# Block-sparse attention and expert layer: sampled value rows of every second group fetched by whole-block transfers, neighbour value rows copied by engines, and a planner with other durations

## The chip, the cores and the metric

The kernel runs on one core of a Trainium2 chip, as one program. Its engines are TensorE (PE, with its weight loads as PEld), VectorE (DVE), ScalarE (ACT), GpSimd (POOL) and SyncE (SP), which here does nothing but issue transfers; 16 DMA engines move the data. Each engine works through its own instructions in the order in which they were written, and waits where one of them waits. The metric is the device time of one execution in microseconds (us).

## The reference

The first half is block-sparse attention over 4 batches of 8 heads, 768 rows in 24 blocks of 32. A row of queries sees its own block and both neighbours, the first and the last block, and three sampled blocks out of a table that comes in as data. The first and the last block of queries see every key.

```
mask = np.abs(blk_i - blk_j) <= 1
mask = mask | (blk_i == 0) | (blk_j == 0) | (blk_i == 23) | (blk_j == 23)
for qb in range(24):
    for kb in sampled_blocks[qb]:
        mask[qb*32:(qb+1)*32, kb*32:(kb+1)*32] = True
attn = softmax(where(mask, scale * q @ k.T, -1e9)) ; out = attn @ v
```

The second half is an expert layer over the 3072 rows of that output (512 wide): a greedy assignment of 384 rows to each of 8 experts by their logits, and `relu(x @ w1[e]) @ w2[e]` for the rows of each.

## The kernel before, in words

The attention runs first (about 340 us of the span), then the choice of the first expert, then the expert layer (class `Moe`). The change is in the attention (class `Attn`) and in the planner (class `Plan`) that sets its order; the instructions of the expert layer keep theirs.

A batch has 24 blocks of queries. Blocks 1 to 22 go in groups of four, u = 0 to 5 (the last has two); the first and the last block go apart (kind "D"), against all keys. In each batch the kernel does this:

- `keys` loads each 128-row chunk of k and q from HBM into a staging tile `st` (SP, L245), transposes it on PE into `S` (L253), and copies it into `kT` or `qT` (ACT or DVE).
- `values` loads v into `vn` (SP, L275) and writes the rows back to HBM as `vrows` (SP, L279), so that they can be fetched by row number.
- `group_keys` puts the keys that a group sees side by side in `kg` (two buffers, used by turns: kg0 for even u, kg1 for odd u): first, last and neighbour blocks by ACT or POOL (L227 on POOL), the sampled blocks by 12 copies on POOL (L338) whose source is a block number read into registers (L333).
- `group_values` puts the values of a group into two tiles: `vw` (two buffers), with the first block and the neighbours, by copies (ACT or POOL) and by transfers from `vn` (SP, L371 to L419); and `vz` (three buffers: u modulo 3), with the sampled blocks, by one indirect gather for each block of queries from `vrows` (POOL, L360: 96 rows of 2080 bytes, by the row numbers in `vidx`), and with the last block (SP, L365). A sampled block that the row sees anyway is fetched from a row of zeros behind `vrows`.
- `pair` multiplies queries with `kg` into `S` (L473; 16 such products are one unit); `unit` takes the smallest and subtracts it (DVE, L514 and L519), transposes (PE, L533), takes the exponential into `aT` (ACT, L539) and multiplies with `vw` and `vz` (PE, L558); `quotient` divides and writes the rows out.

Every piece is a task of `Plan`: a priority (its place on a time scale of 30 to the batch), the engine or engines that may do it with a duration each (microseconds), the tasks it depends on, the buffers it takes, and for a transfer its time on the DMA engines (`move`). `Plan.run` goes through time with these durations and writes each task's instructions when it comes up, so the durations decide the order on every engine and which of ACT, POOL or DVE does a copy. They decide nothing at run time: there each engine takes its instructions in that order, and semaphores hold it until its inputs are there. SP's transfers come out in the planned order too.

Of the kernel before, what the change touches and what calls it, by code (L numbers as in the profile page):

```python
# [24 lines left out]
class Plan:  # L25
# [7 lines left out]
    def __init__(self):  # L33
        self.tasks, self.pools, self.rows = [], {}, {}
# [57 lines left out]
    def run(self, look=0.25, window=9.0):  # L92
# [45 lines left out]
class Attn:  # L138
# [20 lines left out]
    def consts(self):  # L159
# [13 lines left out]
        zero = self.kg[1][0:1].rearrange("p a b c -> p (a b c)")[:, 0:VR]  # L173
        nc.vector.memset(zero, 0.0)
        for b in range(self.nb):
            nc.scalar.dma_start(self.vs[b][S:S + 1], zero)
# [4 lines left out]
    def rows(self):  # L181
# [25 lines left out]
        for r in range(3):  # L207
            sl = slice(32 * r, 32 * r + 32)
            nc.vector.tensor_scalar(row[sl], self.tbl[sl, :, r], float(BS), y[sl], op0=OP.mult, op1=OP.add)
            nc.vector.tensor_scalar(to[sl], row[sl], -1.0, float(S), op0=OP.mult, op1=OP.add)  # L210
            nc.vector.scalar_tensor_tensor(to[sl], had[sl, :, r], 0.5, to[sl], op0=OP.is_ge, op1=OP.mult)
            nc.vector.tensor_tensor(self.vidx[sl], row[sl], to[sl], op=OP.add)
        self.sum4 = T("sum4", [128, E])
# [19 lines left out]
    def keys(self, b, at, ahead):  # L233
# [4 lines left out]
        for (nm, c), n in at:  # L238
# [21 lines left out]
            ld = pl.add(n - ahead, ("SP", 0.5), load, take=[st], move=1.2)  # L260
            self.kld[key] = ld
            a = pl.add(n, ("PE", 0.52), turn, deps=[ld], after=first[nm], take=[ps] + ([] if first[nm] else [sl]), use=[st])
# [3 lines left out]
    def values(self, b, n0, step):  # L266

        nc, pl = self.nc, self.plan
        self.vnslot[b] = s = pl.slot("vn")
        self.rel[b], lds = [], []  # L270
        behind = [] if b else [self.kld[0, "q", 1]]
        vn = self.vn[b % 2]
        for c in range(6):
            def load(c=c):
                nc.sync.dma_start(vn[:, c, :, 0:D], self.v[b, :, 128 * c:128 * c + 128].rearrange("h p d -> p h d"))  # L275
            lds.append(pl.add(n0 + c * step, ("SP", 0.5), load, deps=[self.base], after=lds[:1] + behind, take=[s] if c == 0 else [], use=[s], move=1.2))
            if c % 2:
                def rows(c=c):
                    nc.sync.dma_start(self.vs[b][128 * (c - 1):128 * (c + 1)].rearrange("(c p) x -> p c x", p=128),  # L279
                                      vn[:, c - 1:c + 1].rearrange("p c h d -> p c (h d)"))  # L280
                self.rel[b].append(pl.add(n0 + (c + 1) * step, ("SP", 0.5), rows, deps=lds[-2:], use=[s], move=1.5))
        self.vld[b] = lds

    def group_keys(self, b, u, n):
# [55 lines left out]
        add(("POOL", 0.4 + 0.3 * 3 * len(self.blocks(u))), f)  # L340
        self.kgt[b, u] = ts

    def group_values(self, b, u, n):
# [14 lines left out]
        for g in range(len(bl)):  # L358
# [3 lines left out]
            az(("POOL", 0.95), f, self.rel[b] + [self.idx], move=0.56, late=0.1 * g)  # L362
# [31 lines left out]
        def f():  # L394
            nc.sync.dma_start(vw[32:64, 1], vn[32:64, u])
        aw(("SP", 0.5), f, [u], move=0.2)
# [8 lines left out]
        else:  # L405
# [8 lines left out]
            def f():  # L414
                nc.sync.dma_start(vw[0:32, 2], vn[0:32, u + 1])
            aw(("SP", 0.5), f, [u + 1], move=0.2)

            def f():
                nc.sync.dma_start(vw[0:64, 3], vn[0:64, u + 1])  # L419
            aw(("SP", 0.5), f, [u + 1], move=0.4)  # L420
# [61 lines left out]
    def unit(self, x, n, qs_, avs, avd):  # L482
# [42 lines left out]
        for c0 in range(0, w, 4):  # L525
# [8 lines left out]
            tr = pl.add(n + 1, ("PE", .125 * (c1 - c0) + .02), f, deps=sub, take=[sp], use=[ss])  # L534
# [27 lines left out]
        avd.append(pl.add(n + 2.6, ("PE", 0.66), f, deps=ex + vd + avd, take=[] if s else [avs], use=[sa] + vs, row="AV"))  # L562

    def quotient(self, b, kind, u, m, n, avs, avd):
# [67 lines left out]
        t = pl.add(n + 2, ("PE", .52), f, deps=done, take=[sp], use=[xs])  # L632
# [36 lines left out]
    def run(self, start=None):  # L669
        self.st, self.T, self.ps, self.ev, self.Tslot = {}, {}, {}, {}, {}  # L670
        self.vnslot, self.rel, self.vld, self.vslot, self.vt = {}, {}, {}, {}, {}
        self.kgslot, self.kgt, self.avt, self.xslot, self.xstate, self.fin, self.lgt, self.qd0, self.kld = {}, {}, {}, {}, {}, {}, {}, {}, {}
# [705 lines left out]
def tile_kernel(tc, q, k, v, sampled_blocks, moe_w_gate, moe_w1, moe_w2, out):  # L1378
    nc = tc.nc
    with ExitStack() as ctx:  # L1380
# [10 lines left out]
        with ExitStack() as a:  # L1391
            vs = [dram.tile([S + 1, VR], F32, name=f"vrows{b}") for b in range(B)]
# [32 lines left out]
```

## Time and profile before

| | |
|---|---|
| median of 3 runs | 688.36 us (687.7 to 689.5) |
| profiled execution: its own time | 689.25 us |
| its span, first to last instruction | 687.5 us |
| busy share of the span: PE, DVE, ACT, POOL | 85%, 64%, 51%, 60% |
| mean granted TensorE clock | 0.929 of full speed |
| DMA: bytes moved, packets | 107.57 MB, 126280 |

A row of a timeline begins with the start and the duration in us; in brackets at its end stands how long the engine had stood idle before it and what released it. "issue" means that the profile shows nothing that was waited for. Stretches of equal instructions are merged into one row, x8 meaning eight of them; a merged row lasts from the first start to the last end.

### The profile page before, as it was taken

How to read it: one execution, taken by the hardware profiler on the slowest of the kernel's cores; microseconds unless marked ns; L12 is line 12 of the kernel's file. 1: busy time of each engine (PE TensorE's matmuls, PEld its weight loads, DVE VectorE, ACT ScalarE, POOL GpSimd, SP SyncE). 2: the span in 40 equal slices, each digit the busy share in tenths (PEclk: the TensorE clock that was granted, in tenths of full speed). 3: DMA queues.
4: the chain of work that ended last, by engine and by line, in shares of the span. 5: the costliest groups of instructions: out<-in, count | busy, mean ns of one | idle time of the engine just before them, and what ended most of it. 6: DMA issues, size and time to landing. Idle time of an engine off the chain costs nothing. (4 is left out here: it accounts for less than half of the span.)

```text
span 687.5 us, 19795 instructions
## 1 busy us (share of the span) xinstructions
PE 584.4 (85%) x7416; PEld 443.6 (65%) x7416; DVE 436.8 (64%) x1645; ACT 351.8 (51%) x828; POOL 412.7 (60%) x765
## 2 busy tenths in 40 slices
PE   4768798798988797987613999999999999999996
PEld 2445565475555565564403778878787878889895
DVE  3565576676756668684578787878777787633020
ACT  3644366354634456352443747566665766346341
POOL 4475567546674675856101858576676767867661
PEclk9697999999989999998855999999999999999999
DMA  9999966998599746432103554353635363645301
GB/s 180 239 212 210 259 153 187 212 267 180 139 217 263 176 132 160 121 102 84 62 0 110 182 184 154 129 173 112 213 105 178 111 211 120 201 168 170 126 13 46
DMA packets 126280, 107.57 MB, mean 156 GB/s; under 512 B 81252, under 2 KB 99812, under 8 KB 126184
## 3 DMA queue, kind: packets, MB, share of 16 engines
q1 hardware_dynamic: 116032, 76.05, 42.4%
q0 software_dynamic: 9472, 30.16, 15.3%
q8 instruction: 58, 0.95, 0.6%
q14 instruction: 38, 0.31, 0.1%
q10 hardware_dynamic: 680, 0.10, 0.1%
HBM read 76.38 MB, written 18.98 MB: 139 GB/s over the span
## 5 line engine op out<-in xcount | busy, mean ns | idle before, releaser
L789 POOL TENSOR_TENSOR wlo<-raw,whi 128x512 fp32r<-128x512 f32 x128 | 161.7, 1288 | 57.7 <-ACT whi L789 57.0
L360 POOL DMA_INDIRECT vz<-vrows,vidx x88 | 81.9, 931 | 37.9 <-issue 13.9
L514 DVE TENSOR_REDUCE mn<-S 128x2 f32<-128x512 f32 x88 | 60.1, 684 | 59.7 <-PE S L473 59.6
L539 ACT ACTIVATE aT<-pT 128x512 f32<-128x512 f32 x88 | 51.9, 596 | 71.0 <-PE pT L533 61.3
L338 POOL COPY kg<-kT 128x128 f32 x264 | 63.6, 289 | 33.8 <-issue 27.1
L473 PE MATMUL S<-kg,qT 64*32 64x256 f32 x1408 | 65.5, 419 | 15.3 <-POOL kg L338 13.6
L789 PE MATMUL po<-whi,hh 128*128 128x512 f32 x192 | 77.4, 403 | 0.0
L789 PE MATMUL po<-whi,hl 128*128 128x512 f32 x192 | 76.9, 401 | 0.0
L789 PE MATMUL po<-wlo,hh 128*128 128x512 f32 x192 | 76.5, 398 | 0.0
L789 ACT ACTIVATE whi<-raw 128x512 fp32r<-128x512 f32 x128 | 74.1, 621 | 0.1
L558 PE MATMUL av<-vw,aT 128*32 128x65 f32 x1408 | 53.1, 230 | 11.7 <-issue 7.0
L519 DVE TENSOR_TENSOR s<-S,mn 128x512 f32<-128x512 f32 x88 | 60.4, 687 | 1.8
L789 DVE SCALAR_TENSOR_TENSOR hl<-ph,hh 128x384 fp32r<-128x384 f32 x64 | 35.3, 552 | 39.8 <-ACT hh L789 39.8
L533 PE MATMUL pT<-ident,s 128*128 128x128 f32 x352 | 57.6, 288 | 1.6 <-ACT aTD L539 0.8
L789 PE MATMUL ph<-xhi,whi 128*128 128x384 f32 x256 | 58.4, 345 | 0.4 <-ACT xhi L789 0.3
L789 PE MATMUL ph<-xhi,wlo 128*128 128x384 f32 x256 | 57.9, 343 | 0.0
L789 PE MATMUL ph<-xlo,whi 128*128 128x384 f32 x256 | 57.7, 343 | 0.0
L558 PEld LDWEIGHTS av<-vw,aT 128*32 128x32 f32 x1408 | 33.1, 111 | 34.1 <-issue 21.4
L789 ACT ACTIVATE hh<-ph 128x384 fp32r<-128x384 f32 x64 | 31.2, 487 | 45.6 <-PE ph L789 43.8
L558 PE MATMUL av<-vz,aT 128*32 128x65 f32 x1408 | 49.3, 224 | 2.4 <-issue 1.9
L253 PE MATMUL S<-ident,st 128*128 128x128 f32 x192 | 33.9, 307 | 20.1 <-DMA st<-in_k_dram 9.0
L473 PEld LDWEIGHTS S<-kg,qT 64*32 64x32 f32 x1408 | 25.6, 112 | 38.7 <-POOL kg L338 24.0
(225 smaller groups left out, 1239.4 us busy)
## 6 DMA issues: line engine op xcount, KB each, us to landing
raw<-in_moe_w_dram SPq DMA_DIRECT2D x64, 512.0 KB
vrows<-vn SPq DMA_DIRECT2D x12, 520.0 KB
st<-in_k_dram SPq DMA_DIRECT2D x24, 256.0 KB
st<-in_q_dram SPq DMA_DIRECT2D x24, 256.0 KB
vn<-in_v_dram SPq DMA_DIRECT2D x24, 256.0 KB
xrows<-xt SPq DMA_DIRECT2D x20, 256.0 KB
vw<-vn SPq DMA_DIRECT2D x76, 65.0 KB
vz<-vn SPq DMA_DIRECT2D x12, 260.0 KB
```

Source lines behind the costliest of these rows:

```text
L253: nc.tensor.transpose(ps[:, 128 * p:128 * p + 128], self.st[key][:, 2 * p:2 * p + 2].rearrange("p h d -> p (h d)"), self.ident)
L338: nc.gpsimd.tensor_copy(kg()[:, :, g, 128 + 32 * r:160 + 32 * r], kT()[:, :, bass.ds(pv[3 * g + r] * BS, BS)])
L360: nc.gpsimd.indirect_dma_start(out=vz[0:96, g], out_offset=None, in_=self.vs[b], in_offset=bass.IndirectOffsetOnAxis(ap=self.vidx[:, bl[g] ...
L473: nc.tensor.matmul(x["S"][0][32 * g:32 * g + 32, 256 * j:256 * j + 256], qT[h, p, BS * bl[gi]:BS * bl[gi] + BS], kg[h, p, gi], start=True, ...
L514: nc.vector.tensor_reduce(x["mn"][:, 0:2], x["S"][0].rearrange("p (j y) -> p j y", j=2), axis=AX.X, op=OP.min)
L519: nc.vector.tensor_tensor(x["s"].rearrange("p (j t) y -> p j (t y)", j=2), x["S"][0].rearrange("p (j y) -> p j y", j=2), x["mn"][:, 0:2, N ...
L533: nc.tensor.transpose(ps[:, c - c0], x["s"][:, c], self.ident)
L539: nc.scalar.activation(x["aT"][:, c0:c1], x["ps", c0][:, 0:c1 - c0], AF.Exp, scale=-1.0 if w == 4 else 1.0)
L558: nc.tensor.matmul(av[32 * g:32 * g + 32, 2 * j + s], aT[:, 2 * j + t, 32 * g:32 * g + 32], v[:, gi, h], start=t == 0, stop=t == 1)
L789: return f(*args, **kw)
```

## The change

1. Sampled values of the odd groups (u = 1, 3, 5): instead of a gather for each block of queries on POOL (10 in a batch) SP issues three transfers of a whole sampled block, 32 rows, for each (30 in a batch). The block numbers come from a table `tz` in which a block that is seen anyway is replaced by block 24; they are read into registers on SP once for each group, in the first batch, and kept. Behind `vrows` stand 32 rows of zeros now, not one.
2. Neighbour values: three transfers of SP for a group (two of 32 rows and one of 64) become three copies by ACT or POOL, whichever the planner picks. The transfers of the first block (u = 0 and 1) stay.
3. Loads: of the first batch, the last three chunks of q may start only after `vrows` is written; the first loads of the second batch only after those.
4. The planner: other durations (the gather 1.22 for 0.95, the loads 1.35 for 1.2, and others), 2 us more behind a transfer for what depends on it, a look-ahead of 0.1 for 0.25.

```
         for d in t["deps"]:
-            at = max(at, d["end"])
+            at = max(at, d["end"] + (self.late if d["move"] and d["prio"] > 0 else 0.0))
+        if "SP" in t["eng"] and t["prio"] > 0:
+            at += self.late / 2
...
-    def run(self, look=0.25, window=9.0):
+    def run(self, look=0.1, window=9.0):
...
-            ld = pl.add(n - ahead, ("SP", 0.5), load, take=[st], move=1.2)
+            ld = pl.add(n - ahead, ("SP", 0.5), load, take=[st], move=1.35)
...
-        add(("POOL", 0.4 + 0.3 * 3 * len(self.blocks(u))), f)
+        add(("POOL", 0.8 + 0.245 * 3 * len(self.blocks(u))), f)
...
-        for g in range(len(bl)):
+        for g in range(len(bl)) if u % 2 else ():
+            def f(g=g):
+                if u not in self.kept:
+                    self.kept[u] = nc.values_load_multi_w_load_instructions(
+                        self.tz[0:1, bl[0]:bl[-1] + 1].rearrange("p n r -> p (n r)"), engines=[ET.SP], min_val=0, max_val=NB,
+                        skip_runtime_bounds_check_because="the table is clamped on the chip")[1]
+                for r in range(3):
+                    nc.sync.dma_start(vz[32 * r:32 * r + 32, g], self.vs[b][bass.ds(self.kept[u][3 * g + r] * BS, BS)])
+            az(("SP", 1.6 if b or g else 3.2), f, self.rel[b] + [self.idx], move=0.75, late=0.1 * g)
+        for g in range(len(bl)) if u % 2 == 0 else ():
             def f(g=g):
                 nc.gpsimd.indirect_dma_start(out=vz[0:96, g], out_offset=None, in_=self.vs[b],
                                              in_offset=bass.IndirectOffsetOnAxis(ap=self.vidx[:, bl[g]:bl[g] + 1], axis=0))
-            az(("POOL", 0.95), f, self.rel[b] + [self.idx], move=0.56, late=0.1 * g)
+            az(("POOL", 1.22), f, self.rel[b] + [self.idx], move=0.8, late=0.1 * g)
...
-        def f():
-            nc.sync.dma_start(vw[32:64, 1], vn[32:64, u])
-        aw(("SP", 0.5), f, [u], move=0.2)
+        def f(e):
+            self.copy(e, vw[32:64, 1], vn[32:64, u])
+        aw(both(.62, .64), f, [u])
...
-                nc.sync.dma_start(vw[0:32, 2], vn[0:32, u + 1])
-                nc.sync.dma_start(vw[0:64, 3], vn[0:64, u + 1])
+                self.copy(e, vw[0:32, 2:4], vn[0:32, u + 1, None].to_broadcast([32, 2, VR]))
+                self.copy(e, vw[32:64, 3], vn[32:64, u + 1])
...
+                for c in (2, 3, 4):
+                    self.kld[0, "q", c]["after"].append(self.rel[0][-1])
+                if b == 1:
+                    for t in [self.kld[1, "k", 0], self.vld[1][0]]:
+                        t["after"].append(self.kld[0, "q", 4])
```

Over the program the copies into `vw` go from 27 to 50 on POOL and from 45 to 86 on ACT, the gathers into `vz` on POOL from 88 to 48; SP loses 64 transfers and gains 120. Three places of the new order follow; names are those of the tiles, with buffer numbers where several exist.

PE in the first batch, up to its first product with values (`vw_99`, `vz_101` are those of u = 0, `st` is a staged chunk of k or q). Before:

```order
L473 MATMUL S<-kg_98,qT 32x256 x16
L253 MATMUL S<-ident,st 128x128 x4
L533 MATMUL pT<-ident,s 128x128 x8
L253 MATMUL S<-ident,st 128x128 x4
L533 MATMUL pT<-ident,s 128x128 x4
L473 MATMUL S<-kg_98,qT 32x256 x16
L533 MATMUL pT<-ident,s 128x128 x4
L253 MATMUL S<-ident,st 128x128 x4
L558 MATMUL av<-vw_99,aT 32x65 x4
```

After:

```order
L548 MATMUL pT<-ident,s 128x128 x4
L488 MATMUL S<-kg_98,qT 32x256 x16
L548 MATMUL pT<-ident,s 128x128 x4
L259 MATMUL S<-ident,st 128x128 x4
L573 MATMUL av<-vw_99,aT 32x65 x4
```

Three chunks of the second batch's k stood ahead of the first value product, now one does; one unit of scores (16 products with `kg_98`) and three groups of transposes of `s` moved behind it as well.

POOL in the third batch, between the sampled keys of u = 3 (`kg_98`) and those of u = 4 (`kg_97`); `vz_101` is for u = 3, `vz_102` for u = 4, `vw_100` for u = 3. Before:

```order
L360 DMA vz_101<-vrows_70,vidx 96x520 x4
L227 COPY vw_100<-vn_104 96x520
L227 COPY vw_100<-vn_104 32x520
L360 DMA vz_102<-vrows_70,vidx 96x520 x2
L227 COPY kg_97<-kT 128x4x96
L227 COPY kg_97<-kT 128x4x2x32
L227 COPY kg_97<-kT 128x4x32
L333 TENSOR_LOAD tbl
```

After:

```order
L233 COPY vw_100<-vn_104 96x520
L233 COPY vw_100<-vn_104 64x1040
L233 COPY vw_100<-vn_104 32x520
L375 DMA vz_102<-vrows_70,vidx 96x520
L233 COPY kg_97<-kT 128x4x96
L233 COPY kg_97<-kT 128x4x2x32
L233 COPY kg_97<-kT 128x4x32
L339 TENSOR_LOAD tbl
```

Five of six gathers are gone from in front of the keys of u = 4, and one copy of 64 rows by 1040 is new there.

SP in the first batch, where the second batch's fifth and sixth chunk of k are loaded; before, three transfers of neighbour values (L395 to L419) follow later:

```order
L279 DMA vrows_69<-vn_105 128x2x520
L245 DMA st<-in_k_dram 128x8x64
L275 DMA vn_105<-in_v_dram 128x8x64
L245 DMA st<-in_k_dram 128x8x64
L365 DMA vz_103<-vn_104 32x4x520
L245 DMA st<-in_q_dram 128x8x64
```

After, with `vz_101` now for u = 3 (of its 12 transfers, each behind an ISA row, the first and the last are shown):

```order
L251 DMA st<-in_k_dram 128x8x64
L281 DMA vn_105<-in_v_dram 128x8x64
L367 TENSOR_LOAD tz
L371 ISA
L371 DMA vz_101<-vrows_68 32x520
...
L371 DMA vz_101<-vrows_68 32x520
L285 DMA vrows_69<-vn_105 128x2x520
L251 DMA st<-in_k_dram 128x8x64
```

The sixth chunk of k now stands behind a register load and 12 block transfers.

## Rows read from the trace of the kernel before

**Rows 1.** Busy time of each engine by stretch: the opening, the rest of the first batch, and the three other batches. Columns: stretch, its length, PE, PEld, DVE, ACT, POOL busy us (instructions), granted TensorE clock, mean busy share of the 16 DMA engines, GB/s.

```profile
0.00:55.00 55.00, 33.76 (x364) 22.00 (x364) 27.23 (x67) 25.65 (x57) 31.40 (x92) 0.83 1.01 210
55.00:108.00 53.00, 44.88 (x1099) 31.82 (x1097) 33.13 (x81) 30.73 (x63) 28.03 (x137) 0.92 0.87 199
108.00:186.00 78.00, 68.35 (x1464) 46.09 (x1464) 56.77 (x130) 42.71 (x93) 48.98 (x119) 0.98 0.87 201
186.00:266.00 80.00, 68.91 (x1427) 45.57 (x1428) 52.27 (x118) 38.89 (x82) 50.41 (x121) 0.91 0.81 190
266.00:340.00 74.00, 60.09 (x1368) 39.52 (x1366) 48.70 (x125) 30.96 (x63) 43.06 (x98) 0.91 0.39 109
```

**Rows 2.** Waits of PE's products and weight loads in the first 340 us: who waited for whom, us in total, times, longest.

```profile
PE S L473 <- POOL kg L338: 13.6, 6, 4.2
PE S L253 <- DMA st<-in_k_dram: 9.0, 3, 6.5
PEld S L473 <- POOL kg L338: 24.0, 24, 4.3
PEld av L558 <- ACT aT L539: 8.0, 11, 1.5
```

**Rows 3.** Timeline of PE around its first value product, and the stretch just behind its longest wait (columns as in Rows 1).

```profile
44.97 0.66 PE L253 MATMUL S<-ident,st 128*128 128x128 f32 x4 [1.71 <-DMA st<-in_k_dram]
54.19 1.11 PE L253 MATMUL S<-ident,st 128*128 128x128 f32 x4 [6.51 <-DMA st<-in_k_dram]
55.23 0.44 PE L558 MATMUL av<-vw,aT 128*32 128x65 f32 x8
54.00:60.00 6.00, 5.81 (x132) 3.95 (x132) 1.31 (x4) 1.68 (x3) 2.05 (x9) 0.50 1.09 198
```

**Rows 4.** Timelines of SP and POOL in the opening: the three late loads of q, the last write of `vrows`, the third load of k of the second batch; the sampled keys of u = 1 and the first gather.

```profile
19.02 3.58 SPq L245 DMA_DIRECT2D st<-in_q_dram  x3
31.78 0.58 SPq L279 DMA_DIRECT2D vrows<-vn  x1
39.57 2.89 SPq L245 DMA_DIRECT2D st<-in_k_dram  x1
24.40 2.89 POOL L338 COPY kg<-kT 128x128 f32 x12
35.80 1.13 POOL L360 DMA_INDIRECT vz<-vrows,vidx  x1 [8.52 <-DMA vw<-vn]
```

**Rows 5.** Timeline of POOL in the third batch, from the sampled keys of u = 3 to those of u = 4.

```profile
222.81 2.88 POOL L338 COPY kg<-kT 128x128 f32 x12 [4.04 <-issue]
225.85 0.95 POOL L360 DMA_INDIRECT vz<-vrows,vidx  x1 [0.16 <-issue]
227.10 0.92 POOL L360 DMA_INDIRECT vz<-vrows,vidx  x1 [0.30 <-PE pT L533]
...
234.50 0.62 POOL L227 COPY vw<-vn 32x520 f32<-32x520 f32 x1 [3.40 <-DMA vz<-vrows,vidx]
...
237.60 1.08 POOL L227 COPY kg<-kT 128x384 f32<-128x384 f32 x3
240.05 2.89 POOL L338 COPY kg<-kT 128x128 f32 x12 [1.37 <-issue]
```

**Rows 6.** Timeline of PE: one unit of scores that waited for nothing, then those that waited for sampled keys (u = 4 of the second, third and fourth batch, and u = 1 of the fourth).

```profile
269.80 1.09 PE L473 MATMUL S<-kg,qT 64*32 64x256 f32 x32
160.11 3.18 PE L473 MATMUL S<-kg,qT 64*32 64x256 f32 x32 [0.31 <-POOL kg L338]
240.87 4.04 PE L473 MATMUL S<-kg,qT 64*32 64x256 f32 x32 [3.73 <-POOL kg L338]
314.69 4.04 PE L473 MATMUL S<-kg,qT 64*32 64x256 f32 x32 [4.19 <-POOL kg L338]
276.06 3.53 PE L473 MATMUL S<-kg,qT 64*32 64x256 f32 x32 [3.14 <-POOL kg L338]
```

**Rows 7.** Groups of instructions on POOL and ACT in the first 340 us: shapes xcount, then busy us and mean ns of one, then idle time before them.

```profile
L360 POOL DMA_INDIRECT vz<-vrows,vidx x88 | 81.9, 931 | 37.9 <-issue 13.9 <-DMA vw<-vn 8.5 <-PE av L558 7.0
L227 POOL COPY vw<-vn 32x520 f32<-32x520 f32 x15 | 9.3, 618 | 31.3 <-DMA vz<-vrows,vidx 21.0 <-PE S L253 4.8 <-PE av L558 3.5
L227 POOL COPY vw<-vn 64x1040 f32<-64x1040 f32 x2 | 2.1, 1050 | 7.4 <-PE pT L533 4.8 <-PE pT L649 2.6
L223 ACT ACTIVATE vw<-vn 64x1040 f32<-64x1040 f32 x18 | 19.2, 1068 | 5.9 <-PE av L558 5.7
L223 ACT ACTIVATE vw<-vn 32x520 f32<-32x520 f32 x17 | 10.8, 633 | 0.3
```

**Rows 8.** Timeline of SP in the second batch (the load of the third batch's fifth chunk of k, a transfer of neighbour values) and PE's transpose of that chunk; then the transfers of SP in the expert layer whose address comes from a register, two stretches of four.

```profile
141.04 0.84 SPq L245 DMA_DIRECT2D st<-in_k_dram  x1
146.59 0.55 SPq L419 DMA_DIRECT2D vw<-vn  x1
151.87 0.60 PE L253 MATMUL S<-ident,st 128*128 128x128 f32 x4
400.67 2.23 SPq L1089 DMA_DIRECT2D raw<-in_moe_w_dram  x4
379.77 4.24 SPq L1092 DMA_DIRECT2D raw<-in_moe_w_dram  x4
```

**Rows 9.** Time from the issue of a gather to its landing, over the 88 gathers into `vz`.

```profile
DMA to landing us min/median/max: 3.1/4.8/8.8
```

More of the change, by code (lines that the diff above doesn't have):

```diff
@@ L33, in __init__ @@
     def __init__(self):
-        self.tasks, self.pools, self.rows = [], {}, {}
+        self.tasks, self.pools, self.rows, self.late = [], {}, {}, 2.0
     def pool(self, name, n):
@@ L172, in consts @@
             nc.vector.memset(t[:, :, :, D:D + 1], 1.0)
-        zero = self.kg[1][0:1].rearrange("p a b c -> p (a b c)")[:, 0:VR]
+        zero = self.kg[1][0:BS].rearrange("p a b c -> p (a b c)")[:, 0:VR]
         nc.vector.memset(zero, 0.0)
         for b in range(self.nb):
-            nc.scalar.dma_start(self.vs[b][S:S + 1], zero)
+            nc.scalar.dma_start(self.vs[b][S:S + BS], zero)
         self.wz = cst.tile([128, HP, 32], F32, name="wz")
@@ L212, in rows @@
             nc.vector.tensor_tensor(self.vidx[sl], row[sl], to[sl], op=OP.add)
+        self.tz, tf = T("tz", [1, NB, 3], I32), T("tzf", [1, NB, 3])
+        nc.vector.tensor_scalar(tf, self.tbl[0:1], -1.0, float(NB), op0=OP.mult, op1=OP.add)
+        nc.vector.scalar_tensor_tensor(tf, had[0:1], 0.5, tf, op0=OP.is_ge, op1=OP.mult)
+        nc.vector.tensor_tensor(self.tz, tf, self.tbl[0:1], op=OP.add)
         self.sum4 = T("sum4", [128, E])
@@ L259, in leave @@
                           self.ps[key].rearrange("d (p r) -> d p r", p=HP), 1.0 if nm == "k" else -0.125)
-            ld = pl.add(n - ahead, ("SP", 0.5), load, take=[st], move=1.2)
+            ld = pl.add(n - ahead, ("SP", 0.5), load, take=[st], move=1.35)
             self.kld[key] = ld
-            a = pl.add(n, ("PE", 0.52), turn, deps=[ld], after=first[nm], take=[ps] + ([] if first[nm] else [sl]), use=[st])
+            a = pl.add(n, ("PE", 0.57), turn, deps=[ld], after=first[nm], take=[ps] + ([] if first[nm] else [sl]), use=[st])
             first[nm] = first[nm] or [a]
@@ L275, in load @@
                 nc.sync.dma_start(vn[:, c, :, 0:D], self.v[b, :, 128 * c:128 * c + 128].rearrange("h p d -> p h d"))
-            lds.append(pl.add(n0 + c * step, ("SP", 0.5), load, deps=[self.base], after=lds[:1] + behind, take=[s] if c == 0 else [], use=[s], move=1.2))
+            lds.append(pl.add(n0 + c * step, ("SP", 0.5), load, deps=[self.base], after=lds[:1] + behind, take=[s] if c == 0 else [], use=[s], move=1.35))
             if c % 2:
@@ L280, in rows @@
                                       vn[:, c - 1:c + 1].rearrange("p c h d -> p c (h d)"))
-                self.rel[b].append(pl.add(n0 + (c + 1) * step, ("SP", 0.5), rows, deps=lds[-2:], use=[s], move=1.5))
+                self.rel[b].append(pl.add(n0 + (c + 1) * step, ("SP", 0.5), rows, deps=lds[-2:], use=[s], move=1.8))
         self.vld[b] = lds
@@ L412, in group_values, with f @@
             aw(both(.62, .64), f, [u])
-            def f():
-                nc.sync.dma_start(vw[0:32, 2], vn[0:32, u + 1])
-            aw(("SP", 0.5), f, [u + 1], move=0.2)
-            def f():
-                nc.sync.dma_start(vw[0:64, 3], vn[0:64, u + 1])
-            aw(("SP", 0.5), f, [u + 1], move=0.4)
+            def f(e):
+                self.copy(e, vw[0:32, 2:4], vn[0:32, u + 1, None].to_broadcast([32, 2, VR]))
+            aw(both(1.05, 1.1), f, [u + 1])
+            def f(e):
+                self.copy(e, vw[32:64, 3], vn[32:64, u + 1])
+            aw(both(.62, .64), f, [u + 1])
         self.vt[b, u] = tw + tz
@@ L533, in f @@
                     nc.tensor.transpose(ps[:, c - c0], x["s"][:, c], self.ident)
-            tr = pl.add(n + 1, ("PE", .125 * (c1 - c0) + .02), f, deps=sub, take=[sp], use=[ss])
+            tr = pl.add(n + 1, ("PE", .14 * (c1 - c0) + .02), f, deps=sub, take=[sp], use=[ss])
             def f(c0=c0, c1=c1):
@@ L561, in unit @@
         vd = self.vld[b] if kind == "D" else self.vt[b, u]
-        avd.append(pl.add(n + 2.6, ("PE", 0.66), f, deps=ex + vd + avd, take=[] if s else [avs], use=[sa] + vs, row="AV"))
+        avd.append(pl.add(n + 2.6, ("PE", 0.87 if kind == "D" else 0.56), f, deps=ex + vd + avd, take=[] if s else [avs], use=[sa] + vs, row="AV"))
     def quotient(self, b, kind, u, m, n, avs, avd):
@@ L631, in f @@
                 nc.tensor.transpose(ps[:, p, :], i_.rearrange("p a d -> p (a d)"), self.ident)
-        t = pl.add(n + 2, ("PE", .52), f, deps=done, take=[sp], use=[xs])
+        t = pl.add(n + 2, ("PE", .58), f, deps=done, take=[sp], use=[xs])
         def f(e):
@@ L1391, in tile_kernel @@
         with ExitStack() as a:
-            vs = [dram.tile([S + 1, VR], F32, name=f"vrows{b}") for b in range(B)]
+            vs = [dram.tile([S + BS, VR], F32, name=f"vrows{b}") for b in range(B)]
             Attn(a, tc, q, k, v, sampled_blocks, moe_w_gate, xd, vs, lg, ident).run(start)
```

2 lines of the change are left out of this document (1 added, 1 removed).

## The prediction

> **What bounds the kernel now.** I read the stretches first [rows 1]. In the three later batches PE is busy for 197 of 232 us (85%), and no other engine comes near that (DVE 158, POOL 142, ACT 113). PE takes its instructions in one order, so what it stands idle before its next instruction lengthens the end, and what other engines wait for costs nothing by itself. The DMA engines are the second candidate: their share is 1.01 in the opening and 0.87, 0.87, 0.81 and 0.39 after that.
>
> Then I asked what PE waits for in the first 340 us [rows 2]. Three kinds are large: products of scores for the sampled keys that POOL copies (13.6 us in 6 waits), transposes for a staged chunk of k (9.0 in 3), weight loads for `aT` from ACT (8.0 in 11). The timeline shows where the first two stand. The chunk waits are those of 1.71 and 6.51 us just ahead of the first value product, which starts at 55.23 [rows 3]. Of the key waits, three stand at u = 4: 0.31, 3.73 and 4.19, in batches two to four [rows 6]. One of them costs more than it says. A unit of scores that waits for nothing takes 1.09 us; these took 3.18, 4.04 and 4.04, because the products follow POOL's 12 copies (2.88 us, [rows 5]) one by one; the 24.0 us of weight loads in [rows 2] are this. So u = 4 costs 8.23 of waits and 3.18 + 4.04 + 4.04 − 3 × 1.09 = 7.99 of stretching, **16.2 us**. u = 1 of the fourth batch costs 3.14 + 2.44 = 5.6 in the same way.
>
> A pause has a sequel: in the 6 us from 54, with PE busy for 5.81 of them, the granted clock is 0.50, the lower of the two levels (1.2 GHz) [rows 3]; work that takes 5.8 us there would take 2.9 at the higher.
>
> **The change part by part.**
>
> *POOL loses gathers.* Each is 0.92 to 0.95 us and stands 1.25 us after the one before it [rows 5]; 931 ns is the mean of 88 [rows 7]. I take 1.22. Forty fewer: −48.8 us. It gains 23 copies into `vw`; the three new ones of a group are two of 32 rows and one of 64 × 1040, so 0.62, 0.62 and 1.05 [rows 7], mean 0.76: +17.6. ACT gains 41 such copies at 0.633, 0.633 and 1.068, mean 0.78: +32. POOL is 31 us lighter, ACT 32 us heavier over 340 us, where it was busy for 169 [rows 1]: from 50% to 59%.
>
> *The opening.* Before, PE transposes three chunks of the second batch's k ahead of the first value product, which needs none of them, and waits for the second and the third. After, only the first is left ahead. When are its real inputs there? The last write of `vrows` was issued at 31.78, behind three late loads of q (3.58 us for the three) [rows 4]; those now come after it. Three neighbour transfers ahead of it go and one of the first block is new, at 0.55 each [rows 8] −1.1: it is issued near 27.1. The first gather followed it by 4.0 (31.78 to 35.80, [rows 4]), so gathers start near 31.1, POOL being free: its u = 1 keys ended at 27.3 [rows 4], and the new copies add up to 2.3. The fourth gather is issued 3.7 later, at 34.8, and lands after 4.8 (the median, [rows 9]), at 39.6. PE gets to the product at 55.23 − 8.22 for the two waits − 1.09 for the score unit − 12 transposes of `s` and two chunks' transposes, for which I take the 0.6 to 0.66 of a chunk's four [rows 3, 8], 5 × 0.63 = 3.2: 42.7. The values are there in time, by 3 us. What moved behind the product still has to be done, so the gain is the 8.22 of waits and some 2.4 of low clock: 10.6 at most. Against it: the loads of q and of the second batch's k come later; SP reads registers before its first block transfers; and the DMA engines are full. The third chunk of k, issued at 39.57, was used only at 54.19 [rows 3, 4]; a full set of engines (share 1.01, later 1.09) delays it again wherever it stands. I put 2.6 against it and take **−8**, between −10.6 and 0.
>
> *Keys of u = 4.* In the third batch POOL goes from the end of the keys of u = 3 (225.69) to the start of those of u = 4 (240.05) in 14.4 us [rows 5]: six gathers (7.3), two copies into `vw`, one of which waits 3.40 for the landing of gathers just issued, three key copies and 1.37 before the sampled ones. After: 0.62 + 1.05 + 0.62 for copies, one gather 1.22, key copies 1.08, and 1.4 = 6.0. The keys come 8.4 us earlier. The order on PE, however, now has some 2.6 us less work of its own ahead of this unit; 5.8 us remain, against a cost of 6.7 there (3.73 + 2.95) and 7.1 in the fourth batch. I take 5 in each of these and 2 of the 2.4 in the second: **−12**. Low end −16.2 (all gone); high end −3, if the copies and the reading of registers keep most of the delay: POOL stood 4.04 us before the 12 copies of u = 3 with nothing to wait for [rows 5].
>
> *Keys of u = 1.* The chain on POOL ahead of them is about as long as before, and the unit stands some 5 us earlier on PE: **0**, from −10 (two batches, 5.6 and an estimated 4.9 by the same stretching) to +8 (a second pair of such waits).
>
> *ACT.* The new copies lie in ACT's queue ahead of exponentials. PE's weight loads wait for `aT` for 8.0 us [rows 2] at 50% busy. ACT stays under 60%, so most copies fall into gaps, but one copy of 1.07 us in front of an `aT` is a delay of that size: **+3**, from 0 to +8 (the waits double).
>
> *Copies that stop waiting.* POOL's small copies stood idle for 21.0 us for the landing of gathers [rows 7], since both write values of one group. For odd groups that is gone; for even ones the 64 × 1040 copy still waits. Both lie on POOL beside PE's work; they cost only through the keys, counted above.
>
> *SP.* 120 block transfers come and 64 neighbour transfers go; an odd group of four blocks has 12 in a row, and the loads of the next batch stand behind them. In the second batch a chunk of k was issued at 141.04 and transposed at 151.87 [rows 8]: 10.8 us of lead hide a delay of SP. SP's neighbour transfers cost 0.55 [rows 8]. What one with an address from a register costs is seen only in the expert layer: four in 2.23 (0.56 each) and four in 4.24 (1.06 each) [rows 8]. I take 0.56, since a block of 32 × 520 is of the neighbour transfers' size: 30 × 0.56 − 16 × 0.55 = +8 us of SP in a batch, spread over three groups, inside the lead. Cost **0**; the other end is a rival below.
>
> *DMA bytes* hardly change: the 96 rows of 2080 bytes that a gather fetched come as three blocks of 32 such rows. The neighbour transfers' bytes go.
>
> Sum: −8 − 12 + 0 + 3 = **−17**. The profiled execution took 689.25 us, so 672.3; the median of the runs lies 0.9 below the profiled one: 671.4, and I say 672.
>
> On the gathers a rule speaks against the change. The trace: each holds POOL for 1.22 us until the next, and six stand in front of the keys that PE waits for [rows 5, 6]. The Trainium skill, page "DMA: Bandwidth & Descriptors", section "Issuing engines are not separate DMA queues", says that transfers end up on the same 16 DMA engines whichever engine starts them, and that another issuing engine saves only the time to initiate, usually small beside the transfer. By that rule the move would bring nearly nothing here; by the rows it takes 7.3 us out of a chain of 14.4. No row shows the initiating time as small, so the sum goes by the rows.
>
> **The rivals.**
>
> *More than forecast.* Key waits of u = 4 and u = 1 all vanish and the opening gives 10.6: −10.6 − 16.2 − 10 + 1 = −36, about 653. For it: POOL has 31 us less to do. Against: the planner has also pulled the score units forward.
>
> *Only the opening helps.* Keys stay late, because even groups' copies wait for gathers just issued and registers still take 4 us: −8 + 3 = −5, about 683.
>
> *The DMA engines bound it.* Shares of 1.01 and 0.87 leave little; chunks then arrive when they did, and PE's waits move from keys to chunks. Gain nil: 688. The skill's rule above would end here. Against: PE's waits for transfers behind the opening are under 1 us in all (9.0 less 8.22, [rows 2, 3]).
>
> *Slower: SP becomes the bound.* If a block transfer costs 1.06 us on SP, a batch has 30 × 1.06 − 16 × 0.55 = +23 us there. Ahead of it are 10.8 us of lead: each of the last three batches' chunks then comes up to 12 us late, I take 10, +30 in all, less 17 already won: +13, about 701. It is the whole sum against the forecast when the delay is 5.7 us a batch, that is +16.5 us on SP, at 0.84 us a transfer. For it: each block transfer stands behind an address computation of its own, and the planner allows 1.6 us for three. Against: the 0.56 of the first four.
>
> **How the numbers follow.** About 2 us, 0.3%, is what a measurement of this kernel can tell. Chances: forecast 0.42 (its own range 664 to 680: −8 and −12 each off by some 40% either way), more 0.18, opening only 0.13, DMA-bound 0.09, slower 0.18. Faster is the first three, 0.73; same 0.09; slower 0.18. A range from 651 to 694 holds the forecast, the case of more, both smaller ones, and of the slower case only its mild part; what it leaves out is most of 701's case and a tail below.
>
> **What the profile after would show.** PE's wait for sampled keys falls from 13.6 to under 5, and the u = 4 units are near 1.1 to 2 us long; its wait for chunks falls from 9.0 to under 2; the first value product starts near 43; the attention ends near 323 instead of 340; the weight loads' wait for `aT` stays under 12; block transfers on SP stand 0.56 to 0.6 apart. I am wrong if these are 0.85 or more apart and chunks of k are waited for in batches two to four, if POOL's keys come as late as before behind copies, or if the wait for chunks in the opening only changes its place.

## The result, and the profile after

| | before | after |
|---|---|---|
| median of 4 runs, us | 688.93 | 664.52 (663.4 to 667.75) |
| ratio to before, 95% interval | | 0.965 (0.962 to 0.968) |
| profiled execution, its span, us | 689.25, 687.5 | 663.4, 661.5 |

The kernel is 24.4 us faster; forecast were 16 to 17 (672, range 651 to 694). Four of the experiments below (even copies on ACT, more blocks, and the two with old numbers) ran where the kernel before took 710 us instead of 689, so their times count only as ratios to it. The traces split the 26.0 us by which the spans differ. First both kernels cut at the end of the attention (windows: length, busy us of PE, PEld, DVE, ACT, POOL with instructions, granted clock, DMA share, GB/s). Before:

```profile
0.00:338.11 338.11, 275.30 (x5714) 184.75 (x5714) 216.81 (x508) 168.94 (x355) 201.88 (x563) 0.92 0.78 181
338.11:687.50 349.39, 309.11 (x1702) 258.86 (x1702) 220.02 (x1138) 182.90 (x473) 210.84 (x202) 0.94 0.40 133
```

After:

```profile
0.00:306.22 306.22, 261.59 (x5714) 180.56 (x5714) 208.67 (x515) 193.04 (x389) 188.65 (x549) 0.95 0.74 182
306.22:661.50 355.28, 308.87 (x1702) 258.68 (x1702) 219.95 (x1138) 183.11 (x473) 210.86 (x202) 0.93 0.39 131
```

The attention is 31.9 us shorter, the rest 5.9 us longer. The same 5714 products cost PE 13.7 us less, and it idles 44.6 us, not 62.8. In the 13.7 are the stretched units of u = 4 (8.0) and the clock, and the two overlap, since much of these units ran at the lower level. The clock's records in the trace stand at full or at half; 55.8 us of the attention are at half before (unrounded mean 0.918), 28.3 after (0.954). Second, what PE waits for in the attention after (who waited for whom: us, times, longest; compare [rows 2]):

```profile
PE S L488 <- POOL kg L344: 7.6, 2, 4.7
PE S L259 <- DMA st<-in_k_dram: 11.4, 6, 5.7
PE av L573 <- DVE xt L614: 6.0, 1, 6.0
PE av L573 <- issue: 3.5, 3, 1.6
PEld S L488 <- POOL kg L344: 12.1, 11, 4.8
PEld av L573 <- ACT aT L554: 5.9, 14, 0.7
POOL vw L233 <- DMA vz<-vrows,vidx: 27.6, 10, 6.4
```

5.7 of the 11.4 is the start of the program, which before stands under another name. Waits for keys fell by 6.0 us, those for chunks by 3.3, PE's "issue" pauses over all its lines from 14.5 us (10 of them) to 3.8 (4), and one wait of 6.0, for `xt` (a finished output tile), is new. Third, the places on PE's timeline (compare [rows 3, 6]): first value product, new stalls, u = 1 of the third batch, u = 4 of the third (both units), u = 1 of the fourth, the last score units.

```profile
41.78 0.32 PE L573 MATMUL av<-vw,aT 128*32 128x65 f32 x8
42.55 0.24 PE L573 MATMUL av<-vz,aT 128*32 128x65 f32 x1 [0.34 <-DMA vz<-vrows,vidx]
77.49 0.45 PE L573 MATMUL av<-vw,aT 128*32 128x65 f32 x8 [6.04 <-DVE xt L614]
142.73 0.66 PE L259 MATMUL S<-ident,st 128*128 128x128 f32 x4 [3.12 <-DMA st<-in_k_dram]
176.12 3.50 PE L488 MATMUL S<-kg,qT 64*32 64x256 f32 x32 [2.89 <-POOL kg L344]
215.74 1.09 PE L488 MATMUL S<-kg,qT 64*32 64x256 f32 x32
221.40 1.09 PE L488 MATMUL S<-kg,qT 64*32 64x256 f32 x32
248.42 4.04 PE L488 MATMUL S<-kg,qT 64*32 64x256 f32 x32 [4.68 <-POOL kg L344]
287.93 1.96 PE L488 MATMUL S<-kg,qT 64*32 64x256 f32 x64
```

u = 4 neither waits nor steps behind copies any more. Around the wait for `xt` the clock was at its lower level (columns as in the windows above):

```profile
73.00:83.40 10.40, 5.91 (x104) 4.79 (x108) 5.57 (x17) 2.08 (x5) 6.30 (x83) 0.51 0.99 288
```

How the lead grows is seen at equal progress, the start of PE's next product when n are behind it, after minus before in us:

| n | 400 | 1000 | 1200 | 2000 | 3000 | 3800 | 4000 | 5200 | 5400 | last |
|---|---|---|---|---|---|---|---|---|---|---|
| us | −11.9 | −19.8 | −10.2 | −13.5 | −13.3 | −20.0 | −26.3 | −23.0 | −32.3 | −31.5 |

−11.9 stands just behind the first value product (the 365th before, the 313th after); 10 us are lost again at the wait for `xt` (the 1017th); the steps of −6 and −9 at 3800 and 5200 are u = 4 of the third and fourth batch. The last column is PE's end; the remaining 5.5 us are lost behind it. POOL issues its last write 4.25 us before the end of the span (687.5) in the kernel before:

```profile
683.25 0.97 POOL L789 DMA_INDIRECT out_dram<-ot,idx  x1 [4.38 <-ACT ot L789]
```

and 9.75 us before the end (661.5) after:

```profile
651.75 0.97 POOL L809 DMA_INDIRECT out_dram<-ot,idx  x1 [4.38 <-ACT ot L809]
```

The trace records a closing drain on POOL there, 3.62 us before and 9.13 after; no engine computes any more.

### The profile page after: what moved, and what is told of

The parts are those of the page before. It is cut to its first block, busy times and chain, and to the rows that moved or that the text cites. A ratio compares the mean times of both kernels' runs of the same rounds, so it can differ in the third digit from the quotient of the medians.

```text
span 661.5 us, 20135 instructions
## 1 busy us (share of the span) xinstructions
PE 570.5 (86%) x7416; PEld 439.2 (66%) x7416; DVE 428.6 (65%) x1652; ACT 376.1 (57%) x862; POOL 399.5 (60%) x751
## 3 DMA queue, kind: packets, MB, share of 16 engines
q0 software_dynamic: 6912, 22.17, 10.8%
## 5 line engine op out<-in xcount | busy, mean ns | idle before, releaser
L529 DVE TENSOR_REDUCE mn<-S 128x2 f32<-128x512 f32 x88 | 57.4, 683 | 40.9 <-PE S L488 40.8
L233 POOL COPY vw<-vn 32x520 f32<-32x520 f32 (+3 forms) x50 | 39.9, 798 | 42.8 <-DMA vz<-vrows,vidx 27.6
L229 ACT ACTIVATE vw<-vn 32x520 f32<-32x520 f32 (+3 forms) x86 | 62.8, 730 | 4.2 <-PE av L573 2.2
L488 PE MATMUL S<-kg,qT 64*32 64x256 f32 x1408 | 55.7, 397 | 7.9 <-POOL kg L344 7.6
L534 DVE TENSOR_TENSOR s<-S,mn 128x512 f32<-128x512 f32 x88 | 58.3, 682 | 5.7 <-PE pT L548 5.4
L573 PE MATMUL av<-vw,aT 128*32 128x65 f32 x1408 | 50.9, 229 | 10.4 <-DVE xt L614 6.0
L375 POOL DMA_INDIRECT vz<-vrows,vidx x48 | 44.9, 935 | 12.8 <-issue 8.4
L573 PEld LDWEIGHTS av<-vw,aT 128*32 128x32 f32 x1408 | 31.5, 110 | 27.7 <-issue 14.9
```

What stands on the lines that cost most here:

```text
L229: nc.scalar.activation(o, i, AF.Copy, scale=scale)
L233: nc.gpsimd.tensor_copy(o, i)
L375: nc.gpsimd.indirect_dma_start(out=vz[0:96, g], out_offset=None, in_=self.vs[b], in_offset=bass.IndirectOffsetOnAxis(ap=self.vidx[:, bl[g] ...
L488: nc.tensor.matmul(x["S"][0][32 * g:32 * g + 32, 256 * j:256 * j + 256], qT[h, p, BS * bl[gi]:BS * bl[gi] + BS], kg[h, p, gi], start=True, ...
L529: nc.vector.tensor_reduce(x["mn"][:, 0:2], x["S"][0].rearrange("p (j y) -> p j y", j=2), axis=AX.X, op=OP.min)
L534: nc.vector.tensor_tensor(x["s"].rearrange("p (j t) y -> p j (t y)", j=2), x["S"][0].rearrange("p (j y) -> p j y", j=2), x["mn"][:, 0:2, N ...
```

## The experiments

"Order kept" means that PE and DVE keep the compared kernel's instructions one by one. Kernels that the planner orders anew are named so. Ratios are to the kernel before, run beside each; the changed kernel has 0.965.

**Gathers back on POOL** (changed kernel, order kept).

```
-                for r in range(3):
-                    nc.sync.dma_start(vz[32 * r:32 * r + 32, g], self.vs[b][bass.ds(self.kept[u][3 * g + r] * BS, BS)])
+                nc.gpsimd.indirect_dma_start(out=vz[0:96, g], out_offset=None, in_=self.vs[b],
+                                             in_offset=bass.IndirectOffsetOnAxis(ap=self.vidx[:, bl[g]:bl[g] + 1], axis=0))
```

> The changed kernel with every instruction of PE, DVE and ACT in its new place; only the sampled values of the odd groups are fetched by one gather on POOL again, at the place where SP issued three block transfers. If taking gathers off POOL is what made the keys of u = 4 timely, they come back: 40 x 1.22 = 49 us on POOL, three waits of 2 to 4 us with their stretched score units (up to 16 us), against which SP loses 120 transfers and the two stalls that stand behind them now (6.0 and 3.1 us): about 672, between 668 and 682. If the new order and the earlier loads did it all, the stalls behind SP go and nothing comes back: about 655. The time between POOL's last write and the end, 3.3 us before and 8.8 after, goes back to 3.3 if it hangs on the number of gathers.

721.71 us, ratio 1.047 (1.041 to 1.052): 57 us above the changed kernel. PE's waits:

```profile
PE S L484 <- POOL kg L344: 32.1, 7, 8.2
PE av L569 <- POOL vw L233: 22.0, 7, 6.2
```

Both expectations were too small. The keys come back late, and so do the copies into `vw` that now share POOL's queue. The new order needs the emptier POOL; it isn't better in itself. An order planned for gathers together with neighbour copies was not run.

**Neighbour transfers back on SP** (changed kernel, order kept).

```
-            self.copy(e, vw[32:64, 1], vn[32:64, u])
+            nc.sync.dma_start(vw[32:64, 1], vn[32:64, u])
...
-                self.copy(e, vw[0:32, 2:4], vn[0:32, u + 1, None].to_broadcast([32, 2, VR]))
+                nc.sync.dma_start(vw[0:32, 2], vn[0:32, u + 1])
```

> The changed kernel in its order, but the three neighbour values of a group are fetched by transfers of SP again, at the place of the copies. If the copies only cost ACT and POOL time that PE does not feel, the engines get 50 us back without a gain, and SP gets 64 transfers of 0.55 us more (9 us a batch) in front of what already stalls: 664 to 672. If copies in front of exponentials cost something (the term of +3), it is faster: about 661. If the copies are what made the values timely, it is slower by 10 or more.

685.52 us, ratio 0.995 (0.992 to 0.997), 21 us above the changed kernel:

```profile
PE S L259 <- DMA st<-in_k_dram: 21.7, 8, 5.6
PE av L573 <- DMA vw<-vn: 15.0, 5, 5.0
```

5.6 of the 21.7 is the start of the program. With block and neighbour transfers both in its queue, SP is late for chunks and for `vw`: it is the rival "SP becomes the bound", in this order; block transfers planned without the copies were not run.

**Block transfers alone** (kernel before, order kept; the zero rows and `tz` come along).

```
+                if u % 2:
...
+                    for r in range(3):
+                        nc.sync.dma_start(vz[32 * r:32 * r + 32, g], self.vs[b][bass.ds(self.kept[u][3 * g + r] * BS, BS)])
+                    return
                 nc.gpsimd.indirect_dma_start(out=vz[0:96, g], out_offset=None, in_=self.vs[b],
```

> The kernel before in its old order; only the sampled values of the odd groups come by block transfers on SP instead of gathers on POOL. If POOL's gathers delay the keys of u = 4, most of the 16 us goes: 672 to 676, the opening's waits for chunks stay or grow, since SP reads registers there. If the order is what counts, 688. If SP's queue becomes the bound where the planner does not know of the transfers, chunks of k are waited for in every batch: over 690.

680.49 us, ratio 0.989 (0.983 to 0.996). No wait of PE for POOL's keys is left, in the old order and with no other work moved. That POOL itself is earlier, and not only PE later, its chain in the third batch shows: 8.0 us from the end of the keys of u = 3 to the start of those of u = 4, where it was 14.4 [rows 5].

```profile
217.70 2.88 POOL L342 COPY kg<-kT 128x128 f32 x12 [2.62 <-issue]
228.56 2.89 POOL L342 COPY kg<-kT 128x128 f32 x12 [3.18 <-issue]
```

So the gathers made these keys late. In the place of their waits stand others (5.7 of the 22.5 is the start of the program):

```profile
PE S L257 <- DMA st<-in_k_dram: 22.5, 8, 5.7
PE av L570 <- DMA vw<-vn: 8.1, 5, 4.6
PE av L570 <- DMA vz<-vrows: 5.3, 3, 2.5
```

At product 1200 it stands 9.8 us behind the kernel before, at the last 13.4 ahead: 10 us are lost in the first batch, to SP's transfers, and 23 won behind it, where the waits for keys and most of PE's "issue" pauses are gone. The drain takes 5.5 of it back.

**Both moves, old order** (kernel before as above; the three transfers are copies by ACT at their place).

```
-            nc.sync.dma_start(vw[32:64, 1], vn[32:64, u])
+            self.copy("ACT", vw[32:64, 1], vn[32:64, u])
...
```

> The kernel before in its old order, with the block transfers for the odd groups as above and, besides, the three neighbour transfers of each group as copies by ACT at the same place; planner and loads as before. If the two moves of work help each other (blocks leave POOL free, copies leave SP free), the waits for vw and vz from transfers and for chunks in the run with blocks alone shrink: 670 to 676. If copies that no planner placed stand in front of exponentials, ACT takes the place of SP: 680 to 690. What is left to 664 is then the order's share.

684.27 us, ratio 0.992 (0.989 to 0.995). Waits for chunks are down to 1.2 us, and ACT, which now has all of these copies, has taken their place:

```profile
PE av L570 <- ACT aT L551: 12.8, 7, 3.0
PE pT L545 <- ACT lg L227: 6.1, 2, 3.1
PE S L467 <- ACT qd L227: 5.8, 2, 3.5
```

**Planner and loads alone** (kernel before, planned anew: parts 3 and 4 of the change).

```
+                for c in (2, 3, 4):
+                    self.kld[0, "q", c]["after"].append(self.rel[0][-1])
...
-        add(("POOL", 0.4 + 0.3 * 3 * len(self.blocks(u))), f)
+        add(("POOL", 0.8 + 0.245 * 3 * len(self.blocks(u))), f)
...
```

> The kernel before with the new durations and margins of the planner and the new order of loads, all gathers and neighbour transfers where they were. If the order alone brings the gain, 664 to 668. If it brings the opening alone, 688 - 11 = 677. If the other parts are needed even for that (eight gathers stand in the opening, four for each of the first two groups), 683 to 690.

688.63 us, ratio 0.997 (0.995 to 1.000): no difference that can be measured. The first value product comes at 48.0 instead of 55.2, and the lead is gone again by product 600, with waits for gathers that land late:

```profile
PE av L560 <- DMA vz<-vrows,vidx: 13.0, 5, 5.0
PE S L475 <- POOL kg L340: 8.3, 1, 8.3
```

**The changed kernel without the new loads** (planned anew).

```
-                for c in (2, 3, 4):
-                    self.kld[0, "q", c]["after"].append(self.rel[0][-1])
...
-                    for t in [self.kld[1, "k", 0], self.vld[1][0]]:
-                        t["after"].append(self.kld[0, "q", 4])
```

> The changed kernel, planned anew, without the new order of loads (q's last chunks and the second batch's loads stand where they were before). If the load order is what brings the first value product from 55.2 to 41.8 us, it goes back past 50 and the time is 672 to 678. If it comes from four gathers instead of eight and from the copies, it stays near 42 to 45 and the time is 663 to 668.

668.57 us, ratio 0.973 (0.967 to 0.978). The first value product falls back to 47.1, but with it a wait of 7.38 us for a chunk takes the place of the 6.04 for `xt`; in the profiled execution, the fastest of its four, PE ends 0.8 us from the changed kernel. The ratios differ by 0.8 points, and the intervals touch: that the new loads gain anything is not shown.

**The changed kernel with the old numbers** (planned anew), and **with old numbers and old loads**.

```
-            at = max(at, d["end"] + (self.late if d["move"] and d["prio"] > 0 else 0.0))
+            at = max(at, d["end"])
...
-        add(("POOL", 0.8 + 0.245 * 3 * len(self.blocks(u))), f)
+        add(("POOL", 0.4 + 0.3 * 3 * len(self.blocks(u))), f)
```

> The changed kernel, planned anew with the durations and margins of before (the moved work and the order of loads stay as changed). If the new numbers only describe what the moved work makes possible, 664 to 668. If work moved without them stands in wrong places, as in the run with both moves in the old order (684), 672 to 682.

> The changed kernel with both moves of work as tasks of the planner, but with the planner's durations and margins and the order of loads of before. In the old order itself the two moves gave 0.992 of the time before; with all of the change it was 0.965. If planning the moved work anew (which of ACT and POOL copies, and when) is what makes the difference, the ratio is near 0.965 to 0.975. If the new numbers and loads are needed, each doing for the other, it is 0.98 to 0.995.

688.24 us, ratio 0.971 (0.966 to 0.976), and 687.59 us, ratio 0.968 (0.964 to 0.972). Numbers and loads together are worth 0.3%, within the intervals, as far as ratios to different times of the kernel before can be compared. What both moves gain over the 0.992 of the old order comes from planning them as tasks. Two things change with that: the planner shares the copies between ACT and POOL, and the order on all engines is new. Which of them counts, no run separates.

**Output writes issued by ACT** (changed kernel, order kept).

```
-                nc.sync.dma_start(self.xd[r0 + 128 * u:r0 + 128 + 128 * u], state["x"].rearrange("p h d -> p (h d)"))
+                nc.scalar.dma_start(self.xd[r0 + 128 * u:r0 + 128 + 128 * u], state["x"].rearrange("p h d -> p (h d)"))
```

> The changed kernel in its order, but the 20 writes of a finished output tile to HBM are issued by ACT instead of SP, at the same place. If the 6.0 us that PE loses at 77.5 come from such a write standing behind a register load and 12 block transfers on SP, the wait goes, and with it the low clock behind it (10 us at 1.2 GHz): 655 to 659. If ACT then waits for the tiles in its own queue, or the next chunk is late anyway, 664 or more.

667.4 us, ratio 0.971 (0.965 to 0.976). The wait for `xt` is gone, so its cause is shown: the write of the tile two before stood behind these rows of SP (changed kernel), and behind the 2.5 us in which SP reads block numbers into registers ahead of them:

```profile
64.63 6.21 SPq L371 DMA_DIRECT2D vz<-vrows  x12
70.89 0.42 SPq L285 DMA_DIRECT2D vrows<-vn  x1
71.41 1.49 SPq L251 DMA_DIRECT2D st<-in_k_dram  x1
73.00 0.58 SPq L623 DMA_DIRECT2D xrows<-xt  x1
```

Nothing is gained: the lead of 3.6 us at product 1600 is lost to chunks (14.3 us in 8 waits, where the changed kernel has 5.7 behind its start).

**Values of even groups copied by ACT alone** (changed kernel, order kept).

```
-            self.copy(e, vw[32:64, 1], vn[32:64, u])
+            self.copy(e if u % 2 else "ACT", vw[32:64, 1], vn[32:64, u])
...
```

> The changed kernel in its order, but every copy of values of an even group that the planner gave to POOL is done by ACT, at the same place. On POOL the first of these stands 3 to 6 us for the landing of the gathers just issued (27.6 us in ten waits), with the sampled keys of u = 1 behind it, for which PE waits 2.9 and 4.7 us in the third and fourth batch and then steps behind the copies (2.4 and 3.0 us more). If that wait is what makes these keys late, 13 us go: 652 to 656, less what ACT's 20 us of copies more cost. If it is the reading of block numbers or the chain of key copies, nothing moves: 663 to 667.

703.55 us, ratio 0.991 (0.988 to 0.994): 2.7% above the changed kernel. The cause was right. PE waits for no keys any more, which alone would not show it, as PE itself is later here (first value product at 52.8 us, not 41.8, in the same order); POOL's own chain does. In the changed kernel's third batch it takes 12.2 us from the end of the sampled keys of u = 0 to the start of those of u = 1, with a wait for gathers in it:

```profile
160.19 2.88 POOL L344 COPY kg<-kT 128x128 f32 x12 [3.00 <-DVE s L534]
169.58 2.14 POOL L233 COPY vw<-vn 64x1040 f32<-64x1040 f32 x2 [3.62 <-DMA vz<-vrows,vidx]
175.30 2.89 POOL L344 COPY kg<-kT 128x128 f32 x12 [0.60 <-issue]
```

Here it takes 5.8 us (184.90 to 190.70). The price was wrong: ACT is busy for 220.7 of 346 us, and PE waits for it.

```profile
PE av L573 <- ACT aT L554: 12.8, 8, 2.8
PE pT L548 <- ACT aT L554: 6.7, 3, 3.3
```

**More blocks** (changed kernel, order kept; u = 0 of batches two to four by block transfers too).

```
+                if u == 0 and b:
...
+                    for r in range(3):
+                        nc.sync.dma_start(vz[32 * r:32 * r + 32, g], self.vs[b][bass.ds(self.kept[u][3 * g + r] * BS, BS)])
+                    return
                 nc.gpsimd.indirect_dma_start(out=vz[0:96, g], out_offset=None, in_=self.vs[b],
```

> The changed kernel in its order; in batches two to four u = 0, too, gets its sampled values by block transfers of SP in place of gathers: 9 to 12 transfers (5 to 6 us of SP) more in a batch. If SP has room, u = 1's keys come earlier, as no gather stands before them: 652 to 657. If SP is at its limit (two stalls of 6.0 and 3.1 us stand behind it now), chunks of k are waited for in each batch, 3 to 6 us with their low clock: 666 to 680.

682.85 us, ratio 0.964 (0.959 to 0.969), the same as the changed kernel. Keys for u = 1 are in time, and chunks are late instead, as are the expert layer's logits `lp` that DVE copies:

```profile
PE S L259 <- DMA st<-in_k_dram: 11.1, 4, 7.3
PE pT L683 <- DVE lp L231: 5.6, 3, 4.9
```

**Sixteen gathers more** (changed kernel; between attention and expert layer, into tiles read by nobody).

```
         pl.run()
+        for i in range(16):
+            nc.gpsimd.indirect_dma_start(out=self.vz[i // 4 % 3][0:96, i % 4], out_offset=None, in_=self.vs[3],
...
```

> The changed kernel with 16 more gathers on POOL between attention and expert layer, into tiles that nobody reads any more, where POOL is idle for over 30 us. Of the six kernels so far those with 136 indirect transfers have 3.6 us in POOL's closing drain, those with 96 have 9.1. If the drain hangs on that number, it changes: 6.9 on a straight line between the two, 662; if it hangs on something else of the change, it stays 9.1 and the time 664.5.

680.16 us, ratio 0.988 (0.984 to 0.992). The gathers delay the expert layer's start by 10 us, so the total says nothing; the drain, with nothing else changed, does: 10.44 us instead of 9.13. Over all runs it is 8.15, 9.13, 10.44 us with 36, 48, 64 gathers into `vz` (0.082 us each, a straight line) and 3.61 to 3.63 with 88. Why it falls again there is open.

## Why the prediction was right, and where its steps were off

**Keys of u = 4: right in kind, −16.2 where −12 was taken.** All of the 8.23 of waits and, but for some 0.3 us, the 7.99 of stretching are gone, the low end of the bounds; the run with block transfers alone shows the cause. The chain on POOL that was worked out as 6.0 us, instead of 14.4 [rows 5], is 7.7 (from 203.84 to 211.56):

```profile
200.96 2.89 POOL L344 COPY kg<-kT 128x128 f32 x12 [2.88 <-issue]
203.79 2.42 POOL L233 COPY vw<-vn 96x520 f32<-96x520 f32 x3
206.48 0.94 POOL L375 DMA_INDIRECT vz<-vrows,vidx  x1 [0.27 <-POOL vw L233]
207.47 1.07 POOL L233 COPY kg<-kT 128x384 f32<-128x384 f32 x3
211.56 2.90 POOL L344 COPY kg<-kT 128x128 f32 x12 [3.02 <-issue]
```

POOL stood 3.02 before the last copies for the block numbers, not 1.4. That the copies end at 214.46 and the unit starts at 215.74 shows how little room is left.

**Keys of u = 1: 0 taken, +2.4 measured** (2.89 + 4.68 of waits for 1.98 + 3.14, stretching as before), inside the bounds. The run with even copies on ACT shows the cause: copies on POOL that stand for the landing of gathers make its chain 12.2 us long instead of 5.8.

**The opening: −8 taken, −11.9 reached, beyond the bound of −10.6, and mostly given back.** The last `vrows` was issued at 26.03 (27.1 forecast), the first gather at 33.77 (31.1; POOL was at the keys of u = 1 until 32.69), the product came at 41.78 (42.7). The values came later and PE earlier than worked out, which used up the three us of spare time, and one product waited 0.34 for `vz`. What the 2.6 against it were for was larger: the 6.04 for `xt` with its low clock took 10 us. Without the new loads the opening is 5 us later and PE's end 0.8.

**SP: 0 taken; the step that failed.** A block transfer costs SP 6.21 / 12 = 0.52 us in the row of twelve above (0.56 taken), and the lead of 10.8 us was measured at a load of k. But "the loads of the next batch stand behind them" left out what else stands in that queue: the writes of finished tiles, whose buffer DVE needs again. That cost 6.0 us, as the run with the output writes on ACT shows, and probably the 3.12 for a chunk in the second batch. (PE's waits for transfers behind the opening, put at under 1 us in the prediction, were 1.8 in the kernel before with those for `vw` and `vz`.) In the run with both kinds of transfers this rival decides, and the output writes on ACT or more blocks only change which of SP's transfers is late.

**ACT: +3 taken, nothing measured**, with the copies shared by the planner (weight loads wait 5.9 us for `aT`, before 8.0). The 41 new copies cost ACT 26.5 us (32 taken), the 23 new ones POOL 22.3 (17.6); ACT is busy for 193 of 306 us, 63% and not under 60. With more copies on it (64%) the kernel is 2.7% slower: so ACT's share does not tell the term; which copy stands in front of which exponential probably does.

**Left out: pauses and drain.** PE's "issue" pauses fell by 10.7 us; the prediction does not mention them. Before and with planner and loads alone they are 14.5 and 15.2 us, with block transfers alone 1.9, with gathers back (and neighbour copies) none. But in four runs without the neighbour transfers and with fewer gathers they are there again: 20.0 us (even copies on ACT), 14.0 (more blocks), 19.9 and 17.8 (old numbers, without and with old loads), mostly of 0.3 to 0.5 us each. What PE stands for in them no view shows, and whether the moves removed them stays open. The drain took 5.5 back. So a sum that was short by 15 in the attention came out 8 off in all: the kind of the gain was foreseen, but that the total lies so near the forecast is in part luck, since one thing left out hides half of another. The terms told here add up to some 23 of the 31.9 us (−16.2 + 2.4 − 11.9 + 10 + 3.1 − 10.7); the other 9 are put down to no one place.

**Signs.** The first value product, u = 4, `aT` and the spacing on SP came about as foretold. PE's wait for keys (7.6, under 5 foretold), its wait for chunks (5.7 without the start, under 2) and the end of the attention (306, 323) did not; and a wait of the opening did change its place, to `xt`, though the lead it cost was less than the lead won.

The rule of the Trainium skill that the prediction weighed ("DMA: Bandwidth & Descriptors", section "Issuing engines are not separate DMA queues"), that another issuing engine saves only the time to initiate, usually small, would have given nearly no gain. With gathers back on POOL in the same order the kernel is 57 us slower; here the issuing engine's time decides, as PE waits 32.1 us for POOL's keys and 22.0 for its copies. That the engines end up sharing the DMA engines was no limit: the share in the attention fell from 0.78 to 0.74.

## What to carry to other kernels

When work moves from one queue to another, list everything that stands behind its new place, writes whose buffer is reused as well as loads, and not only the load with the nearest due time. Two moves can need each other: block transfers without the copies gave 1.1% in the old order and 0.5% in the new one, because the queue that takes the work becomes late; copies without the block transfers were 4.7% slower in the new order; both together gave 2.7 to 3.5% only when the planner could place them. Neither move alone was planned anew, so what it would give then is open. When every further shift only renames the wait (keys, chunks, `aT`), as in the last runs here, the engines seem to be in balance; that less work would help from there on was not tried.

## What the runs showed of the hardware

The closing drain of POOL is part of the time and hangs on the number of its indirect transfers: 8.15 to 10.44 us with 84 to 112 in all, 3.6 with 136. PE's pauses in which it waits for nothing that is shown add up to 14.5 and 15.2 us in the two kernels with 88 gathers and the neighbour transfers, to 0 to 5.3 in eight runs where one or both are gone, and to 14.0 to 20.0 in four others of that kind; what they hang on is open.
